# A gated linear attention with a two-layer feed-forward block: w_in issued behind a v tile, w_out in four rows a partition, turned q copied straight, and a new order

## The chip, the cores and the metric

The kernel runs on one core of a Trainium2 chip. The metric is the time of one execution on the device in microseconds (us). Three runs of the kernel before gave 192.94, 193.02 and 193.77 us, so its median is 193.02 us. One further execution was recorded by the hardware profiler; its own time was 192.63 us.

## The reference

There are four sequences (B = 4), eight heads (H = 8), 768 steps (S) and 48 numbers a head (D). For each sequence and head a 48 x 48 state is carried through the steps:

```python
f = 1.0 / (1.0 + np.exp(-f_logit))
for t in range(S):
    state = f[:, :, t, :, None] * state + np.einsum('bhd,bhe->bhde', k[:, :, t], v[:, :, t])
    y[:, :, t] = np.einsum('bhd,bhde->bhe', q[:, :, t], state)
x = y.transpose(0, 2, 1, 3).reshape(B * S, H * D)     # 3072 x 384
h = x @ w_in                                          # 3072 x 2048
out = np.maximum(0.01 * h, h) @ w_out                 # 3072 x 384
```

All inputs and the output are float32 in device memory.

## The kernel before, in words

**Tiling.** The 768 steps are cut into six chunks of 128. A unit is one chunk of one sequence, so there are 24 units, numbered chunk by chunk: units 0 to 3 are the first chunk of the four sequences. Inside a chunk the recurrence becomes matmuls. The logarithms of the gates are summed along the chunk by a triangular matmul; k and q are scaled by the exponentials of that sum; k and q are turned, so that the head's numbers lie on the partitions; k against q gives scores, which are masked to the past and multiplied with v. The state of all earlier chunks is added through another matmul and is then brought up to date. The resulting y is turned to x, and two units together (256 columns) go through the feed-forward block: `up(m, g, bk)` makes two of the 16 blocks of 128 hidden numbers for the pair m, `up_act` applies the leaky rectifier into the buffer gT, `down(u, half, bk)` multiplies half of the hidden blocks of unit u with w_out, `put` copies the result out of PSUM and `out_dma` stores it. Line 412 is the matmul of `up` and line 422 that of `down`.

**The first chunk.** Units 0 to 3 are treated as one "quad", by functions whose names begin with `q_`. Their f, k and q lie in the tiles fq, kq and qq, with four consecutive steps of a head next to each other in a partition (`load_quad`, line 69), and a partition holds every fourth row for one sequence. Each of the twelve loads has 192 KB. The quad is worked in two halves hh of four heads. `q_exp_act` and `q_ln_act` make the log gates on ScalarE, `q_gate_pe` (line 202) sums them, `q_decay_act` (line 206) takes the exponentials into emq and aq, and `q_k_scale` and `q_q_scale` (line 211) scale k and q into khq and qhq on VectorE or GpSimd. `q_turn_pe` (line 223) turns them on TensorE; `q_k_out` and `q_q_out` copy the turned tiles from PSUM to kTq and qTq and undo the four-step interleaving while they copy. `q_score_pe` (line 240) multiplies them. `q_mask` (line 251), or `q_wf_act` with `q_mask_pool`, masks the scores; `q_back_pe` and `q_back_out` turn k back for the state; `q_mix_pe` (line 257) makes y, `state_pe` (line 379) with `q_state_dve` (line 282) the state, and `y_out`, `x_pe`, `x_out` bring y into the feed-forward block's input xT.

**Loads.** Raw tiles of later units (f, k, q, v; 192 KB each, in runs of 48 float32) are issued by `load_part` (line 166) on the SP queue, in the written order; an issue that has to wait holds up all issues behind it. w_in and w_out are cast from float32 to bf16 on the way and are therefore issued from GpSimd's software queue, w_in in two halves of its columns (`load_w_in`, line 175) and w_out in four quarters of its rows (`load_w_out`, line 180). An issue on GpSimd stands in line with GpSimd's computing instructions.

**The order** of all instructions is written out by hand at the end of the function, one call a line; each engine works through its own instructions in that order, and the framework adds the waits. `idle_pe(n, bk)` (line 139) issues n matmuls on zeros. The letters V, A and G in a call mean VectorE, ScalarE and GpSimd.

Of the kernel before, what the change touches and what calls it, by code (L numbers as in the profile page):

```python
# [16 lines left out]
def kernel(  # L17
# [37 lines left out]
    def bank(i):  # L55
        return banks[i][:, :]
# [47 lines left out]
    w_in_b = const.tile([128, NK, FF], BF16, tag="w_in")  # L104
    w_out_b = const.tile([128, NF, KD], BF16, tag="w_out")
# [83 lines left out]
    qTq = [const.tile([128, 2, 4, 128], BF16, name=f"qTq{i}", tag=f"qTq{i}") for i in range(2)]  # L189
# [35 lines left out]
    def q_turn_out(dst, hh, bk, pp):  # L225
        tp = bank16(bk).rearrange("p (a j t b) -> p a b t j", a=2, j=4, b=4)
        return dict(out=dst[hh][:, pp].rearrange("p b (t j) -> p b t j", j=4), in_=tp[:, pp])

    def q_k_out(eng, hh, pp, bk):
        move(eng, **q_turn_out(kTq, hh, bk, pp))  # L230

    def q_q_out(eng, hh, pp, bk):
        move(eng, **q_turn_out(qTq, hh, bk, pp))

    def q_score_pe(hh, bp, bk0, bk1):
        pw = [bank(bk).rearrange("p (b a n) -> p b a n", b=2, a=2) for bk in (bk0, bk1)]
        for bl in range(2):
            for pp in range(2):
                for e in range(2):
                    nc.tensor.matmul(pw[e][:, bl, pp, :], kTq[hh][64 * e:64 * e + 64, pp, 2 * bp + bl, :],  # L240
                                     qTq[hh][64 * e:64 * e + 64, pp, 2 * bp + bl, :], start=True, stop=True)
# [166 lines left out]
    def up(m, g, bk):  # L408
        for i in range(2):
            for kk in range(NK):  # L410
                ff = 2 * g + i
                nc.tensor.matmul(bank(bk)[:, i * 256:(i + 1) * 256], w_in_b[:, kk, ff * 128:(ff + 1) * 128],  # L412
# [21 lines left out]

    q_exp_act(0)
    q_exp_act(1)
    q_ln_act(0)
    load_part(1, "v", v)
    q_ln_act(1)
    load_part(0, "v", v)  # L440
    load_w_in(0)
    idle_pe(40, 7)
    q_gate_pe(0, 0, 0)
    load_part(3, "v", v)
    load_w_in(1)
    q_gate_pe(0, 1, 1)
    load_part(2, "v", v)
    q_decay_act(0, 0, emq, 1.0, 0)
    q_gate_pe(1, 0, 2)
    q_decay_act(0, 0, aq, -1.0, 0)  # L450
    q_k_scale(V, 0, 0)
    q_decay_act(0, 1, emq, 1.0, 1)
    q_gate_pe(1, 1, 3)
    q_q_scale(G, 0, 0)
    q_decay_act(0, 1, aq, -1.0, 1)
    q_k_scale(V, 0, 1)
    q_decay_act(1, 0, emq, 1.0, 2)
    q_turn_pe(khq, 0, 0, 4)
    q_decay_act(1, 0, aq, -1.0, 2)
    q_end_pe(5)  # L460
    q_q_scale(V, 0, 1)
    load_part(4, "f", f_logit)
    q_k_scale(G, 1, 0)
    q_decay_act(1, 1, emq, 1.0, 3)
    q_turn_pe(khq, 0, 1, 4)
    q_q_scale(V, 1, 0)
    q_decay_act(1, 1, aq, -1.0, 3)
    q_turn_pe(qhq, 0, 0, 6)
    q_k_out(A, 0, 1, 4)
    q_k_scale(G, 1, 1)  # L470
    q_turn_pe(qhq, 0, 1, 6)
    q_k_out(V, 0, 0, 4)
    q_end_act(5)
    q_turn_pe(khq, 1, 0, 7)
    q_q_out(A, 0, 0, 6)
    q_turn_pe(qhq, 1, 0, 0)
    q_q_out(V, 0, 1, 6)
    q_q_scale(G, 1, 1)
    q_turn_pe(khq, 1, 1, 7)
    cast_v(V, 1)  # L480
    q_score_pe(0, 1, 1, 2)
    q_k_out(A, 1, 0, 7)
    q_k_out(V, 1, 1, 7)
    q_score_pe(0, 0, 3, 5)
    q_mask(0, 1, 0, 1)
    q_wf_act(0, 1, 1, 2)
    q_turn_pe(qhq, 1, 1, 0)
    q_back_pe(1, 4)
    q_wf_act(0, 0, 1, 5)
    load_part(4, "k", k)  # L490
    q_back_pe(3, 6)
    q_q_out(V, 1, 1, 0)
    q_mask_pool(0, 1, 1)
    q_back_pe(0, 7)
    q_q_out(A, 1, 0, 0)
    q_back_pe(2, 2)
    q_back_out(V, 1, 4)
    q_back_out(A, 3, 6)
    q_mask(0, 0, 0, 3)
    q_mask_pool(0, 0, 1)  # L500
    q_back_out(A, 2, 2)
    idle_pe(4, 1)
    q_score_pe(1, 0, 1, 5)
    cast_v(V, 0)
    q_back_out(A, 0, 7)
    state_pe(1, 0)
    q_score_pe(1, 1, 4, 6)
    q_mask(1, 0, 1, 5)
    q_mask(1, 0, 0, 1)
    state_pe(0, 3)  # L510
    q_mask(1, 1, 0, 4)
    idle_pe(5, 5)
    q_mix_pe(0, 2)
    q_mask(1, 1, 1, 6)
    q_mix_pe(1, 7)
    load_part(4, "q", q)
    y_out(A, 0, 2)
    y_out(V, 1, 7)
    q_state_dve(0)
    idle_pe(6, 4)  # L520
    x_pe(0, 5)
    x_pe(1, 1)
    cast_v(G, 3)
    load_part(4, "v", v)
    x_out(A, 0, 5)
    q_state_dve(1)
    q_state_pool(0)
    x_out(A, 1, 1)
    idle_pe(5, 7)
    q_mix_pe(3, 4)  # L530
    load_part(5, "f", f_logit)
    state_pe(3, 6)
    q_state_pool(1)
    up(0, 0, 2)
    y_out(A, 3, 4)
    cast_v(V, 2)
    q_state_dve(3)
    load_w_out(1)
    load_part(5, "k", k)
    up(0, 7, 7)  # L540
    up_act(0, 0, 2)
    load_w_out(0)
    q_mix_pe(2, 3)
    x_pe(3, 5)
    load_part(5, "q", q)
    up_act(0, 7, 7)
    state_pe(2, 0)
    y_out(V, 2, 3)
    up(0, 4, 1)
    q_state_pool(3)  # L550
    x_out(A, 3, 5)
    q_state_dve(2)
    up(0, 6, 4)
    load_w_out(3)
    up_act(0, 4, 1)
    x_pe(2, 6)
    gate_exp(4)
    up(0, 1, 2)
    q_state_pool(2)
    x_out(V, 2, 6)  # L560
    up_act(0, 6, 4)
    load_part(5, "v", v)
    up(0, 3, 7)
    load_w_out(2)
    gate_ln(4)
    up_act(0, 1, 2)
    up(1, 1, 3)
    up_act(0, 3, 7)
    up(1, 7, 5)
    up_act(1, 1, 3)  # L570
    up(1, 6, 0)
    up_act(1, 7, 5)
    up(1, 5, 1)
    up_act(1, 6, 0)
    load_part(6, "f", f_logit)
    cast_v(V, 4)
    gate_pe(4, 6)
    up(1, 3, 4)
    up_act(1, 5, 1)
    decay_em(4, 6)  # L580
    up(1, 2, 2)
    decay_a(4, 6)
    k_scale(V, 4)
    up(1, 0, 7)
    up_act(1, 3, 4)
    q_scale(G, 4)
    up_act(1, 2, 2)
    up(0, 5, 3)
    up_act(1, 0, 7)
    up(0, 2, 5)  # L590
    load_part(6, "k", k)
    up_act(0, 5, 3)
    turn_pe(4, 0)
    gate_exp(5)
    up(1, 4, 1)
    up_act(0, 2, 5)
    turn_k(V, 4, 0)
    gate_ln(5)
    turn_q(V, 4, 0)
    down(2, 0, 6)  # L600
    up_act(1, 4, 1)
    down(1, 0, 4)
    load_part(6, "q", q)
    gate_pe(5, 2)
    down(3, 0, 7)
    decay_em(5, 2)
    decay_a(5, 2)
    k_scale(V, 5)
    down(0, 0, 3)
    load_part(6, "v", v)  # L610
    q_scale(V, 5)
    load_part(7, "f", f_logit)
    state_pe(4, 5)
    state_dve(4)
    turn_pe(5, 0)
    load_part(7, "k", k)
    down(1, 1, 4)
    turn_k(A, 5, 0)
    turn_q(V, 5, 0)
    load_part(7, "q", q)  # L620
    cast_v(V, 5)
    score_pe(2, 1, 2, 5, 0)
    put(A, 1, 4)
    load_part(7, "v", v)
    down(0, 1, 3)
    mask(5, 0, 5)
    gate_exp(6)
    out_dma(1)
    gate_ln(6)
    mask(4, 1, 2)  # L630
    state_pe(5, 4)
    down(2, 1, 6)
    mask(4, 0, 1)
    put(A, 0, 3)
    load_part(8, "f", f_logit)
    mask(5, 1, 0)
    out_dma(0)
    gate_pe(6, 5)
    state_dve(5)
    mix_pe(4, 2)  # L640
    put(A, 2, 6)
    cast_v(G, 6)
    mix_pe(5, 3)
    decay_em(6, 5)
    load_part(8, "k", k)
    state_pool(4)
    y_out(V, 4, 2)
    down(3, 1, 7)
    decay_a(6, 5)
    y_out(V, 5, 3)  # L650
    out_dma(2)
    gate_exp(7)
    k_scale(V, 6)
    gate_ln(7)
    state_pool(5)
    load_part(8, "q", q)
    x_pe(4, 1)
    q_scale(V, 6)
    x_pe(5, 0)
    put(A, 3, 7)  # L660
    state_pe(6, 6)
    load_part(8, "v", v)
    x_out(V, 4, 1)
    x_out(A, 5, 0)
    gate_pe(7, 4)
    state_dve(6)
    turn_pe(6, 2)
    decay_em(7, 4)
    out_dma(3)
    up(2, 3, 5)  # L670
    decay_a(7, 4)
    turn_k(V, 6, 2)
    k_scale(G, 7)
    load_part(9, "f", f_logit)
    turn_q(A, 6, 2)
    cast_v(V, 7)
    up(2, 6, 3)
    q_scale(V, 7)
    up_act(2, 3, 5)
    load_part(9, "k", k)  # L680
    up(2, 0, 7)
    up_act(2, 6, 3)
    turn_pe(7, 1)
    gate_exp(8)
    load_part(9, "q", q)
    state_pe(7, 0)
    up_act(2, 0, 7)
    up(2, 4, 6)
    turn_k(V, 7, 1)
    load_part(9, "v", v)  # L690
    gate_ln(8)
    turn_q(V, 7, 1)
    up(2, 2, 4)
    state_dve(7)
    up_act(2, 4, 6)
    load_part(10, "f", f_logit)
    up(2, 1, 2)
    up_act(2, 2, 4)
    score_pe(3, 5, 3, 7, 1)
    load_part(10, "k", k)  # L700
    up_act(2, 1, 2)
    gate_pe(8, 6)
    up(2, 5, 0)
    mask(6, 1, 3)
    load_part(10, "q", q)
    decay_em(8, 6)
    cast_v(G, 8)
    decay_a(8, 6)
    up(2, 7, 4)
    mask(7, 0, 7)  # L710
    k_scale(G, 8)
    up_act(2, 5, 0)
    load_part(10, "v", v)
    down(4, 0, 2)
# [607 lines left out]
```

## Time and profile before

| what | value |
|---|---|
| median of three runs | 193.02 us |
| profiled execution, own time | 192.63 us |
| span of the profiled execution, first to last instruction | 190.8 us |
| mean granted TensorE clock | 0.982 |
| TensorE busy | 175.7 us (92%) |
| VectorE busy | 87.4 us (46%) |
| ScalarE busy | 124.1 us (65%) |
| GpSimd busy | 59.2 us (31%) |
| read from and written to device memory | 25.17 MB and 4.72 MB |

A row of the profile's groups names a line, an engine, an operation, the tiles out and in, the shape, how often it ran, its busy time and the mean length of one. Matmuls are pipelined, so the mean length of one (273 ns at line 412) is longer than the distance from one to the next. The chain of work that ended last is followed back from the last instruction; each piece of it has a start, a length and what ran. The slices cut the span into 40 equal parts of 4.77 us, each digit the busy share in tenths. Rows of busy time by window give start and end, the window's length, busy time and instructions of TensorE, its weight loads, VectorE, ScalarE and GpSimd, then the granted clock, the busy share of the 16 DMA engines and GB/s.

### The profile page before, as it was taken

To read this page: it belongs to the slowest core of one execution; us is meant where nothing else is said; L and a number is where in the kernel's file an instruction comes from. 1 tells how busy PE (TensorE), PEld (TensorE's weight loads), DVE (VectorE), ACT (ScalarE), POOL (GpSimd) and SP (SyncE) were. 2 spreads that over 40 slices of the span, in tenths; PEclk is the share of its full clock that TensorE was granted. 3 is DMA by queue.
4 is the path that set the end of the run, shared out by engine and by line. 5 is a ranking of instruction groups with operands and counts; after the bars stand their busy time and mean duration, and the time that the engine had idled before them with its cause. 6 is when DMAs were issued, how large, how long until landed. Compare 5 with 4: busy or idle time off the path is not lost.

```text
span 190.8 us, 4830 instructions
## 1 busy us (share of the span) xinstructions
PE 175.7 (92%) x1905; PEld 136.3 (71%) x1905; DVE 87.4 (46%) x193; ACT 124.1 (65%) x266; POOL 59.2 (31%) x109
## 2 busy tenths in 40 slices
PE   4952679999999999999999999999999999999992
PEld 2841459886679778768877787877668787776861
DVE  7001799313597557547556436894528304010000
ACT  2661176994479879967968778986458665642822
POOL 8000855620143644441532512844502500000000
PEclk9997599999999999999999999999999999999999
DMA  4999899999088989899999999972742490113202
GB/s 143 264 222 259 172 190 213 166 185 178 25 196 190 212 176 235 167 228 200 217 193 192 221 195 191 227 157 65 156 115 62 79 138 0 45 43 83 82 3 84
DMA packets 106679, 29.42 MB, mean 154 GB/s; under 512 B 97696, under 2 KB 105888, under 8 KB 106656
## 3 DMA queue, kind: packets, MB, share of 16 engines
q1 hardware_dynamic: 102656, 25.18, 62.2%
q0 software_dynamic: 2912, 3.15, 10.1%
q10 hardware_dynamic: 1088, 0.79, 1.3%
q8 instruction: 15, 0.25, 0.5%
q14 instruction: 8, 0.07, 0.1%
HBM read 25.17 MB, written 4.72 MB: 157 GB/s over the span
## 4 chain that ended last, share of the span: by engine, by line
PE 84%; DMA 9%; ACT 2%; SPq 1%; DVE 1%; issue 1%; POOL 1%; POOLq 0%; ACTq 0%
PE ps L412 33%; PE ps L422 33%; DMA qq<-in_q_dram 6%; PE ps L332 3%; PE ps L357 3%; DMA fq<-in_f_logit_dram 2%; PE ps L371 2%; PE ps L368 2%; PE ps L304 2%; PE ps L379 2%; PE ps L402 2%; SPq L69 1%; PE ps L139 1%; PE ps L223 1%; ACT kqh L145 1%
## 5 line engine op out<-in xcount | busy, mean ns | idle before, releaser
L412 PE MATMUL ps<-xT,w_in_b 128*128 128x256 bf16 x576 | 70.6, 273 | 0.0
L422 PE MATMUL ps<-w_out_b,gT 128*128 128x384 bf16 x384 | 68.4, 326 | 0.0
L417 ACT ACTIVATE gT<-ps 128x512 bf16<-128x512 f32 x96 | 56.8, 604 | 12.3 <-PE ps L412 10.2
L412 PEld LDWEIGHTS <-w_in_b 128*128 128x128 bf16 x576 | 54.3, 98 | 7.7
L422 PEld LDWEIGHTS <-gT 128*128 128x128 bf16 x384 | 36.2, 98 | 20.6
L361 DVE TENSOR_TENSOR wm<-ps,ut 128x512 bf16<-128x512 f32 x40 | 24.9, 682 | 14.7 <-ACT gT L417 10.4
L288 POOL CAST sb<-sf 64x192 bf16<-64x192 f32 x40 | 15.1, 378 | 35.9 <-PE ps L368 31.3
L145 ACT COPY osb<-ps 128x384 f32<-128x384 f32 x23 | 11.0, 480 | 20.7 <-PE ps L422 20.7
L319 DVE TENSOR_TENSOR kqh<-k_raw,em_t 128x384 bf16<-128x384 f32 x14 | 7.9, 567 | 12.9 <-ACT em_t L311 12.7
L323 POOL TENSOR_TENSOR kqh<-q_raw,a_t 128x384 bf16<-128x384 f32 x11 | 10.3, 938 | 10.4 <-issue 7.1
L393 POOL TENSOR_TENSOR sf<-sf,a_end 128x192 f32<-128x192 f32 x16 | 9.2, 576 | 13.1 <-DVE sf L388 12.6
L147 DVE CAST xn<-ps 128x384 bf16<-128x384 f32 x12 | 6.5, 554 | 12.6 <-ACT osb L145 7.8
L311 ACT ACTIVATE em_t<-ps 128x384 bf16<-128x384 f32 x20 | 9.8, 497 | 2.5 <-PE ps L307 2.5
L147 DVE COPY kqT<-ps 128x512 bf16<-128x512 bf16 x17 | 6.8, 421 | 8.6 <-PE ps L332 5.3
L298 ACT ACTIVATE lf<-f_raw 128x384 bf16<-128x384 f32 x20 | 10.5, 532 | 0.1
L145 ACT COPY kqT<-ps 128x512 bf16<-128x512 bf16 x11 | 6.3, 587 | 6.6 <-PE ps L332 3.8
L295 ACT ACTIVATE f_raw<-f_raw 128x384 f32<-128x384 f32 x20 | 10.4, 526 | 0.0
L139 PE MATMUL ps<-fill 128*128 128x256 bf16 x60 | 9.2, 317 | 1.1 <-DVE ind L129 1.1
L314 ACT ACTIVATE a_t<-ps 128x384 bf16<-128x384 f32 x20 | 9.9, 508 | 0.0
L145 ACT CAST xn<-ps 128x384 bf16<-128x384 f32 x12 | 5.8, 480 | 4.7 <-PE ps L371 2.9
L387 DVE TENSOR_TENSOR sf<-sf,ps 64x192 f32<-64x192 f32 x16 | 5.5, 342 | 7.1 <-PE ps L379 4.2
L139 PEld LDWEIGHTS <-fill 128*128 128x128 bf16 x60 | 6.7, 114 | 2.8 <-issue 1.3
(88 smaller groups left out, 194.1 us busy)
## 6 DMA issues: line engine op xcount, KB each, us to landing
v_raw<-in_v_dram SPq DMA_DIRECT2D x24, 192.0 KB, 4.0
out_dram<-osb SPq DMA_DIRECT2D x24, 192.0 KB, 2.5
f_raw<-in_f_logit_dram SPq DMA_DIRECT2D x20, 192.0 KB, 3.9
k_raw<-in_k_dram SPq DMA_DIRECT2D x20, 192.0 KB, 4.0
q_raw<-in_q_dram SPq DMA_DIRECT2D x20, 192.0 KB, 4.0
w_in_b<-in_moe_w_in_dram POOLq DMA_DIRECT2D x2, 768.0 KB, 12.2
w_out_b<-in_moe_w_out_dram POOLq DMA_DIRECT2D x4, 384.0 KB, 8.6
qq<-in_q_dram SPq DMA_DIRECT2D x4, 192.0 KB, 12.1
```

The source lines that it names most:

```text
L139: nc.tensor.matmul(bank(bk)[:, 0:256], fill[:, 0:128], fill[:, 0:256], start=True, stop=True)
L145: eng.copy(out=out, in_=in_)
L147: eng.tensor_copy(out=out, in_=in_)
L288: nc.gpsimd.tensor_copy(out=state_b[b][r, :, e * D:(e + 1) * D], in_=state_f[b][r])
L295: nc.scalar.activation(raw[u]["f"], raw[u]["f"], AF.Exp, scale=-1.0)
L298: nc.scalar.activation(lfs[u % R_LF][:, :, 0:D], raw[u]["f"], AF.Ln, bias=1.0)
L314: nc.scalar.activation(a_ts[u % R_EM], bank(bk)[:, 0:H * D], AF.Exp, scale=-1.0)
L323: eng.tensor_mul(qhs[u % R_KQS][:, :, 0:D], r["q"], a_ts[u % R_EM])
L361: nc.vector.tensor_mul(wms[e][u % R_WM], bank(bk).rearrange("p (i n) -> p i n", i=P2), ut[:, None, :].to_broadcast([128, P2, 128]))
L412: nc.tensor.matmul(bank(bk)[:, i * 256:(i + 1) * 256], w_in_b[:, kk, ff * 128:(ff + 1) * 128], xTs[m % R_XT][:, kk].rearrange("p a n -> p ...
L417: nc.scalar.activation(gTs[m % GBUFS][:, 2 * g:2 * g + 2].rearrange("p f a n -> p (f a n)"), bank(bk), AF.Prelu, alpha=0.01)
L422: nc.tensor.matmul(bank(bk)[:, 0:KD], gTs[u // 2 % GBUFS][:, ff, u % 2, :], w_out_b[:, ff, :], start=(ff == 0), stop=(ff == NF - 1))
```

## The change

Six things change together.

1. **First loads.** The loads of k for sequences 2 and 3 move from ScalarE's queue to SP's, and ScalarE loads its activation table right after its two loads of f.
2. **w_in.** `load_w_in(0)` stood right behind the first activations in the written order, the first thing in GpSimd's queue after the constants. Now a new instruction, `touch('v')`, copies one column of the raw v tile of unit 1 on GpSimd; it waits for that tile, and both issues of w_in stand behind it. The v tiles of the first chunk are now issued in the order 2, 0, 1, 3.
3. **Turned q.** `q_q_out` copies a turned q from PSUM as it lies; the interleaving of the four steps is undone by the stride with which the score matmuls read q.
4. **w_out.** A partition takes four consecutive rows of w_out in each quarter, where it took one row of each of four blocks.
5. **w_in's columns.** To match, `up` takes every fourth column of w_in as the weights of a matmul, where it took 128 neighbouring ones.
6. **Order.** The hand-written order is new throughout: the second half of heads comes first, all four units of the first chunk come before the first `up`, and the fillers are 52 where there were 60.

```diff
     first_load(nc.sync, "k", 0)
-    first_load(nc.scalar, "k", 2)
+    nc.scalar.preload_act_table_set("natural_log_exp_and_others")
     first_load(nc.sync, "k", 1)
-    first_load(nc.scalar, "k", 3)
+    first_load(nc.sync, "k", 2)
+    first_load(nc.sync, "k", 3)
     first_load(nc.sync, "q", 0)
-    nc.scalar.preload_act_table_set("natural_log_exp_and_others")
...
+    w_in_p = w_in_b.rearrange("p a (g n i) -> p a g n i", n=128, i=4)
...
+    seen = const.tile([128, 1], FP32, tag="seen")
+
+    def touch(what):
+        src = {"f": fq[:, 0, 0, 0:1], "k": kq[:, 0, 0, 0:1], "q": qq[:, 0, 0, 0:1],
+               "v": raws["v_raw"][1][:, 0, 0:1], "w": raws["v_raw"][3][:, 0, 0:1]}[what]
+        nc.gpsimd.tensor_copy(out=seen, in_=src)
...
-                            in_=moe_w_out.rearrange("(a p) n -> p a n", p=128)[:, g * w:(g + 1) * w, :])
+                            in_=moe_w_out.rearrange("(g p i) n -> p g i n", p=128, i=w)[:, g, :, :])
...
-    qTq = [const.tile([128, 2, 4, 128], BF16, name=f"qTq{i}", tag=f"qTq{i}") for i in range(2)]
+    qTq = [const.tile([128, 2, 512], BF16, name=f"qTq{i}", tag=f"qTq{i}") for i in range(2)]
...
     def q_q_out(eng, hh, pp, bk):
-        move(eng, **q_turn_out(qTq, hh, bk, pp))
+        move(eng, qTq[hh][:, pp], bank16(bk).rearrange("p (a n) -> p a n", a=2)[:, pp])
...
+                    nc.tensor.matmul(bank((bk0, bk1)[e])[:, i * 128:(i + 1) * 128], kTq[hh][r, pp, b, :],
+                                     qTq[hh][r, pp].rearrange("p (j t b) -> p b t j", j=4, b=4)[:, b], start=True, stop=True)
...
-                nc.tensor.matmul(bank(bk)[:, i * 256:(i + 1) * 256], w_in_b[:, kk, ff * 128:(ff + 1) * 128],
+                nc.tensor.matmul(bank(bk)[:, i * 256:(i + 1) * 256], w_in_p[:, kk, ff // 4, :, ff % 4],
```

The start of the new order, as GpSimd and SP see it:

```diff
+    load_part(2, "v", v)
+    load_part(0, "v", v)
+    load_part(1, "v", v)
+    load_part(3, "v", v)
+    q_q_scale(G, 1, 0)
...
+    q_q_scale(G, 0, 0)
+    q_q_scale(G, 0, 1)
+    cast_v(G, 2)
+    touch('v')
+    cast_v(G, 1)
+    load_w_in(0)
+    load_w_in(1)
+    q_mask_pool(1, 1, 1)
+    q_mask_pool(0, 1, 1)
...
+    up(1, 3, 7)
```

More of the change, by code (lines that the diff above doesn't have):

```diff
@@ L623 @@
[L623 to L641 removed]
+    put(A, 0, 1)
+    down(1, 1, 3)
+    cast_v(V, 5)
+    turn_q(A, 5, 0)
+    turn_k(V, 5, 0)
+    out_dma(0)
+    gate_exp(6)
+    state_pe(5, 2)
@@ new lines @@
+    load_part(11, "k", k)
+    decay_a(8, 4)
+    down(4, 0, 3)
+    mask(6, 0, 0)
+    k_scale(G, 8)
+    up_act(2, 5, 2)
+    q_scale(V, 8)
+    load_part(11, "q", q)
+    mix_pe(6, 1)
+    mask(7, 1, 7)
+    cast_v(G, 9)
+    state_pe(8, 5)
+    load_part(11, "v", v)
+    down(4, 1, 3)
+    mask(7, 0, 6)
+    state_pool(6)
+    y_out(A, 6, 1)
+    gate_exp(10)
+    state_dve(8)
+    load_part(12, "f", f_logit)
+    gate_ln(10)
+    x_pe(6, 4)
+    turn_pe(8, 0)
+    put(A, 4, 3)
+    x_out(V, 6, 4)
@@ L937 @@
[L937 to L958 removed]
+    load_part(17, "k", k)
+    up(4, 1, 7)
@@ new lines @@
+    up_act(4, 2, 2)
+    turn_q(V, 12, 3)
+    mix_pe(10, 4)
+    gate_ln(14)
+    turn_k(V, 12, 3)
+    load_part(17, "q", q)
+    state_pe(11, 1)
+    cast_v(G, 15)
+    up_act(4, 1, 7)
+    down(6, 0, 6)
+    mask(11, 1, 5)
+    state_pool(10)
+    y_out(A, 10, 4)
+    state_dve(11)
+    load_part(17, "v", v)
+    gate_ln(15)
+    down(8, 0, 0)
+    load_part(18, "f", f_logit)
+    x_pe(10, 2)
+    load_part(18, "k", k)
+    down(6, 1, 6)
+    x_out(A, 10, 2)
+    load_part(18, "q", q)
+    gate_pe(13, 3)
@@ new lines @@
+    turn_q(V, 15, 1)
+    turn_k(A, 15, 1)
+    down(11, 0, 5)
+    up_act(6, 5, 0)
+    score_pe(7, 4, 3, 7, 2)
+    up(6, 0, 6)
+    mask(15, 0, 7)
+    state_pe(15, 1)
+    up(6, 6, 0)
+    mask(15, 1, 2)
+    gate_exp(19)
+    cast_v(G, 19)
+    up_act(6, 0, 6)
+    cast_v(G, 18)
+    up(6, 7, 7)
+    state_dve(15)
+    up_act(6, 6, 0)
+    mix_pe(15, 2)
+    mask(14, 0, 4)
+    gate_exp(18)
+    down(12, 0, 6)
+    up_act(6, 7, 7)
+    state_pool(15)
+    y_out(V, 15, 2)
+    gate_ln(18)
+    mask(14, 1, 3)
@@ new lines @@
+    gate_pe(16, 1)
+    x_pe(15, 0)
+    down(12, 1, 6)
+    decay_em(16, 1)
+    x_out(V, 15, 0)
+    gate_ln(19)
+    k_scale(V, 16)
+    decay_a(16, 1)
+    mix_pe(14, 4)
+    load_part(22, "k", k)
+    q_scale(V, 16)
+    put(A, 12, 6)
+    gate_pe(18, 7)
+    state_pe(16, 2)
+    state_pool(14)
+    y_out(A, 14, 4)
+    down(10, 0, 3)
+    out_dma(12)
+    decay_em(18, 7)
+    state_dve(16)
+    load_part(22, "q", q)
+    decay_a(18, 7)
+    k_scale(V, 18)
+    x_pe(14, 0)
+    q_scale(G, 18)
@@ new lines @@
+    turn_pe(16, 1)
+    x_out(A, 14, 0)
+    gate_pe(17, 6)
+    down(11, 1, 5)
+    turn_k(V, 16, 1)
+    turn_q(A, 16, 1)
+    turn_dma(18)
+    decay_em(17, 6)
+    decay_a(17, 6)
+    k_scale(V, 17)
+    up(7, 7, 4)
+    put(A, 11, 5)
+    q_scale(G, 17)
+    load_part(23, "k", k)
+    up(7, 5, 2)
+    up_act(7, 7, 4)
+    out_dma(11)
+    state_pe(17, 7)
+    up(7, 6, 0)
+    load_part(23, "q", q)
+    up_act(7, 5, 2)
+    state_dve(17)
+    turn_pe(17, 1)
+    up_act(7, 6, 0)
+    up(7, 2, 6)
@@ new lines @@
+    turn_k(V, 17, 1)
+    turn_q(A, 17, 1)
+    up(7, 4, 5)
+    up_act(7, 2, 6)
+    up(7, 3, 4)
+    up_act(7, 4, 5)
+    score_pe(8, 2, 7, 0, 1)
+    up_act(7, 3, 4)
+    up(7, 0, 6)
+    mask(17, 0, 0)
+    down(13, 0, 5)
+    mask(16, 1, 7)
+    cast_v(G, 21)
+    up_act(7, 0, 6)
+    cast_v(G, 20)
+    gate_exp(21)
+    mask(16, 0, 2)
+    gate_exp(20)
+    up(7, 1, 4)
+    mask(17, 1, 1)
+    gate_ln(21)
+    state_pe(18, 0)
+    gate_ln(20)
+    mix_pe(16, 6)
+    state_dve(18)
+    up_act(7, 1, 4)
@@ new lines @@
+    down(10, 1, 3)
+    state_pool(16)
+    y_out(A, 16, 6)
+    x_dma(16)
+    mix_pe(17, 7)
+    put(A, 10, 3)
+    down(15, 0, 2)
+    state_pool(17)
+    y_out(A, 17, 7)
+    out_dma(10)
+    x_dma(17)
+    gate_pe(19, 1)
+    down(15, 1, 2)
+    decay_em(19, 1)
+    decay_a(19, 1)
+    k_scale(V, 19)
+    gate_pe(21, 4)
+    q_scale(G, 19)
+    gate_pe(20, 0)
+    put(A, 15, 2)
+    down(14, 0, 6)
+    decay_a(20, 0)
+    out_dma(15)
+    decay_a(21, 4)
+    turn_dma(19)
+    q_scale(V, 20)
@@ new lines @@
+    mix_pe(23, 5)
+    y_out(V, 22, 0)
+    up(10, 4, 7)
+    y_out(A, 23, 5)
+    x_dma(22)
+    up(10, 1, 1)
+    up_act(10, 4, 7)
+    x_dma(23)
+    up(10, 5, 4)
+    up_act(10, 1, 1)
+    up(10, 6, 2)
+    up_act(10, 5, 4)
+    up(9, 3, 6)
+    up_act(10, 6, 2)
+    down(20, 0, 3)
+    up_act(9, 3, 6)
+    down(21, 0, 0)
+    down(19, 0, 5)
+    down(18, 0, 7)
+    down(19, 1, 5)
+    down(18, 1, 7)
+    put(A, 19, 5)
+    out_dma(19)
+    down(20, 1, 3)
+    put(A, 18, 7)
+    out_dma(18)
```

1303 lines of the change are left out of this document (550 added, 753 removed).

## The prediction

> **What bounds the kernel now.** I read the page's busy slices first, then the chain that ended last, the DMA queues in two windows of the start, the busy times by window, and last the groups of TensorE and VectorE that the change touches.
>
> The slices: TensorE is full from the seventh slice (one is 4.77 us) to the end, and the clock is granted in full there. What can be won lies in the first 31 us.
>
> ```profile
> PE   4952679999999999999999999999999999999992
> DVE  7001799313597557547556436894528304010000
> PEclk9997599999999999999999999999999999999999
> DMA  4999899999088989899999999972742490113202
> ```
>
> The chain in order of time (start, length, what): TensorE, VectorE and GpSimd stand still for q. It is asked for up to 7.25 and has landed at 19.28.
>
> ```profile
> 7.25 12.03 DMA qq<-in_q_dram
> ...
> 24.72 0.68 DVE wm L251
> ...
> 31.44 1.31 PE ps L412 x12
> ...
> 34.77 3.93 PE ps L412 x36
> ```
>
> DMA queues, first from 5 to 10 us, then from 10 to 15 us (packets, MB, share of 16 engines): the software queue q0, which carries only w_in here, takes over half and then five sixths of the engines.
>
> ```profile
> q0 software_dynamic: 234, 0.48, 53.8%
> ...
> q0 software_dynamic: 401, 0.79, 84.1%
> ```
>
> With 32.2% from 15 to 20 us, w_in costs 2.69 + 4.21 + 1.61 = 8.5 us of all 16 engines (4.25 a half), inside the wait for q. The same view gives other prices: 0.75 MB of quads in the first 5 us took 49.9% of them, 2.5 us, so four quad tiles (0.79 MB) cost 2.6 us; from 20 to 31 us a raw tile costs 1.0 us (2.13 MB in 98.5% of 11 us); w_out from 31 to 46 us costs 71.7% of 15 us, 10.75 us.
>
> Busy times by window: after q has landed VectorE is the pace, 10.14 of 11.2 us. Then TensorE has no gap.
>
> ```profile
> 14.00:20.00 6.00, 1.02 (x24) 0.85 (x24) 1.62 (x4) 0.67 (x2) 0.55 (x1) 0.76 1.06 237
> 20.00:31.20 11.20, 9.22 (x133) 7.54 (x134) 10.14 (x19) 5.62 (x11) 7.13 (x9) 0.82 0.99 194
> 31.20:46.00 14.80, 14.80 (x154) 12.55 (x151) 4.90 (x12) 11.90 (x25) 6.47 (x13) 1.00 1.20 184
> ```
>
> **The change, part by part.** Profiled run: span 190.8, own time 192.63, so 1.83 lies around the span; the median of the runs, 193.02, is 0.39 above it.
>
> *q without w_in.* First data moves at 2.3 us; f, k and q cost 3 x 2.6 = 7.8 us of the engines and then end at about 10.1. The last q is issued at about 7.3 to 7.9 (SP now issues two k tiles more, but its q issue waited for f until 4.96 anyway) and a first-load tile took 3.9 us to land: 11. So q lands at 10 to 11 instead of 19.28, and it no longer decides: the decays on ScalarE (L206) start at 10.11, because the gate matmuls follow the 40 idle matmuls and these stay. Their third ends at 10.86 + 0.50 = 11.36, and there VectorE can scale q. ScalarE's table load moves ahead, which gains nothing behind those matmuls.
>
> *VectorE's way to the first up.* In the new order all four first units are finished before the first `up`, so more stands on VectorE ahead of it. From 11.4, by rows: four scalings at 0.55 = 2.2; casts of v0 and v3 at 0.36 = 0.7; two turned k at 0.68 = 1.4; two turned q, now straight, at 0.41 as the straight kqh copy = 0.8 (0.69 before, so 0.55 is saved on this chain); six masks at 0.68 = 4.1; states of two units at 0.75 = 1.5; y of units 2 and 0 at 0.55 = 1.1; x of unit 2 at 0.36. Sum 12.2, and 0.65 of waiting for ScalarE's copies of the same tiles: the first `up` could start at 24.2. ScalarE and GpSimd lie beside it: GpSimd scales q until 14.3 (0.92 each, the third when its decay ends at 13.28), casts v2 and v1, and masks from 17.3 (2 x 1.15, done at 19.6, before the matmuls that need them at 20.5).
>
> *The wait in front of w_in.* `touch` needs v1, the third v tile in SP's order. SP issues the v tiles from 8 us on, each when a k tile has landed; four cost 4 us of the engines and land from 12 to 14, so the wait itself is about hidden behind GpSimd's scaling. Queued behind it on GpSimd are the cast of v1, both w_in issues (0.93 and 0.78), two masks and w_out. The first w_in issue comes at 15.6. In the profile 1.9 us passed from issue (3.07) to packets; then a half takes 4.25/0.85 = 5.0 us at the share that q0 had (84.1% here, 89.1% when w_out ran against raw tiles from 36 to 40 us), and about 0.8 to land: 23.3 and 28.3. The first half is needed at 24.2, the second by the seventh `up`, 6 x 0.66 later: 28.2. So w_in just fits. At a share of 60% (71.7 of 71.7 + 47.1, q0 and q1 from 31 to 46 us) a half takes 7.1 us, the second lands at 32.5, and 4.2 us are lost. Ends 0 and 4.2; I take 1.5, nearer the first, since two rows speak for it.
>
> *w_out, four rows a partition.* Four times fewer and longer pieces. Bounds: 10.75 us as now, or 8.5 us, w_in's price for as many bytes. It is issued from about 28, behind w_in. The first `down` comes 15 `up` and 0.9 of other matmuls after the first, at 36 to 37; two quarters at 4.25/0.85 land at about 35 to 36, the rest at 40, when the second halves start. Lost: 0 to 2, taken 0.5.
>
> *w_in in steps of four.* 576 weight loads now read every fourth column, and 576 times anything counts. Loads of neighbouring columns, one after another, come every 28 ns (16 of L264 in 0.51 us, the last 0.096) and hide below matmuls that come every 109 ns (6 in 0.66). The nearest row for a step is VectorE's copy: 0.68 stepped, 0.41 straight, 1.65 times. 28 x 1.65 = 46 ns hides: cost 0. The other end takes the recorded 98 ns as the price: 162, 53 over, times 576 = 30 us. I take 0, as the spacing shows what a load really holds up; no row excludes the other end.
> The Trainium skill has two rules here. "Advanced Engine Details and Errata", Memory Cachelines, says that SBUF is read in 16-byte lines and needs two hits on a line: a step of four bf16 still makes two, so by it the sum stays as it is; no run here shows it yet. "TensorE: Matmul & The Clock Gate", Weight-path perf modes, has the fast weight load also for stepped columns; without it a load takes by that page an estimated 107 ns (128/1.2), which the 109 ns still cover.
>
> *Turned q in steps.* The 32 score matmuls (L240, 8 in 0.40 us) read q 256 bytes apart. At 1.65 times it is +0.26 a call; the first call is on the way, others lie below masks: 0 to 1.0, taken 0.3.
> By the same Cachelines section one hit on a line pays, by an amount that it does not state: the rule speaks against this edit, and the term would be above 0, as taken.
>
> *The sum.* At 34.60 before, 24 `up` matmuls and all of the first four units are done, one gate (0.4) is not; the last matmul ends at 187.4: 152.8 later. After the first `up` of the new order there remain 152.8 + 24 x 0.109 + 0.17 (one x) - 0.4 = 155.2, then 3.4 of copying and storing: 158.6. The old equivalent start is 190.8 - 158.6 = 32.2. The new: 24.2 + 1.5 + 0.5 + 0.3 = 26.5. Span 185.1, own time 186.9, against the median of runs 187.3. The rest of the order has the same matmuls, up to 8 idle ones fewer; I cost it at nothing, since TensorE is gapless in both halves of the profile; if the new order leaves gaps, nothing covers them.
>
> **The rivals.**
> *DMA is the next bound.* Now w_in, w_out and raw tiles follow each other closely. Up to 46 us the engines worked 12.2 + 6.4 + 11.1 + 17.8 = 47.5 us (share times window) and had then loaded everything through unit 7. The new kernel needs 45.2 of it by 46 - 5.7 = 40.3, while 38 us at 1.1 give 42. If this stops TensorE, 3.4/1.1 = 3 us go back, or w_in at 60% does the same: 190 to 192. Against it: unit 7 is first used at 55, and at 46 to 56 the share fell to 0.45.
> *w_in comes much too late and the change does nothing.* If the halves take 7.1 us and w_out loses its 2, with 1 for the scores: 24.2 + 7.2 = 31.4, 192.2. Speaks for it: the old halves needed 10.2 and 14.1 us to land; against it: that was with quads beside them on two queues.
> *Slower: the stepped weights show.* The place is L412, the price (load - 109 ns) x 576; it cancels the gain of 5.7 at 119 ns a load, and at 162 ns gives 217. For it: the recorded 98 ns; against it: the spacing of 28.
>
> **How the numbers follow.** Half a per cent, 1 us, is about what these runs can tell from no change. My forecast (184.0 to 189.8) 0.58; DMA bound (189.8 to 192) 0.17; no gain 0.06; slower 0.19, of which 0.13 for the weights and 0.06 for gaps in the new order. Faster 0.75, same 0.06, slower 0.19. The range 184 to 192 leaves out the slower cases and the equal ones' upper part; its low end is no stall at all (24.2, 185.0) and 1 us for earlier loads.
>
> **What would show it.** q landing by 11; VectorE scaling q at 11.4; w_in's landings near 23 and 28; first L412 at 24 to 26, with gaps in front of the seventh `up` if w_in is late; L412 still at 0.66 us for 6; L240 above 0.40 for 8; q0 with some 1536 fewer packets. L412 at over 0.70 for 6 or gaps on TensorE after 40 us would make it wrong.

## The result, and the profile after

The changed kernel takes 195.24 us (median of four runs, 194.94 to 195.56), the kernel before 193.06 us beside it. The ratio is 1.0105, with a 95% interval of 1.0081 to 1.013: slower by about 1%, where 187.3 us was forecast. The profiled execution took 195.56 us, its span 193.8 us. Medians and ranges here and below are of all runs of a kernel; the ratios leave out the few runs that took over 1.5% longer than the fastest of the same kernel.

The slices of the page, as shown for before (one is now 4.85 us):

```profile
PE   4988956999999999999999999999999998999992
DVE  6058981022474694878158418526228705100000
PEclk9999995799999999999999999999999999999999
DMA  5998999993498989799998997670491263202202
```

TensorE's hole has become shallower and has moved. Before, it stood in the third and fourth slice (10 to 19 us) and waited for q. Now it stands in the sixth and seventh (24 to 34 us), and in the seventh and eighth (29 to 39 us) the granted clock falls as well. The chain in order of time (start, length, what) names the cause:

```profile
17.17 0.88 POOL w_in_b L183
18.05 12.78 DMA w_in_b<-in_moe_w_in_dram
30.87 1.25 PE ps L418 x5
32.13 0.32 PE ps L408 x3
32.45 7.81 PE ps L418 x54
...
156.50 3.01 PE ps L418 x28
159.51 2.34 DMA xT<-xn
161.98 3.44 PE ps L418 x30
```

L418 is the matmul of `up` (L412 before). Where the chain ran through q's loading until 19.28, it now runs through w_in's second half until 30.83. Behind it 54 matmuls take 7.81 us, 145 ns each, where 36 took 3.93 us before, 109 ns each. Late in the kernel there is a stop that the old order did not have, for two turns by DMA. The timeline shows the moment of the wait (start, busy time, what; in brackets the idle time before and what ended it):

```profile
26.72 0.27 PE L418 MATMUL ps<-xT,w_in_b 128*128 128x256 bf16 x1
...
30.87 0.78 PEld L418 LDWEIGHTS <-w_in_b 128*128 128x128 bf16 x5 [4.24 <-DMA w_in_b<-in_moe_w_in_dram]
30.87 1.25 PE L418 MATMUL ps<-xT,w_in_b 128*128 128x256 bf16 x5 [3.88 <-DMA w_in_b<-in_moe_w_in_dram]
```

The issues of w_in and the time to landing (the first half is issued at 17.1 us and lands at 26.3, the second at 18.0 and 30.8):

```profile
L183 POOL DMA_DIRECT2D w_in_b<-in_moe_w_in_dram x2: 786/862/937, 17.1 to 18.0; - x2
...
DMA to landing us min/median/max: 9.2/11.0/12.8
```

One matmul of the first `up` runs, and the second one waits four microseconds. The first `up` reads hidden blocks 6 and 7, which lie in the first half of w_in; that half had landed, as the first matmul proves. The built kernel's list of instructions on TensorE tells why: the second weight load waits for the second half's semaphore (DMASW1), a counter that this transfer raises when it has landed. In the kernel before, that wait stands in front of the seventh pair of load and matmul, the first that reads the second half.

```
487 L418 Ldweights w_in_b [waits DVE_49,DMASW0_49]
488 L418 Matmult ps_71<-xT_217,w_in_b 128x256 [waits Activation_49]
489 L418 Ldweights w_in_b [waits DMASW1_49]
490 L418 Matmult ps_71<-xT_217,w_in_b 128x256
```

In a partition's row of 6144 elements of w_in_b, the second half's pieces begin at 1024 and end at 6143, with pieces of the first half between them. The first weight load reads every fourth element from 514 to 1022, ahead of all of them; the second reads from 2562 to 3070, between them, and touches none. This fits a framework that compares a stepped read with a transfer by their two ends alone; no run tests that.

Three parts of the profile are as forecast. q landed 4.0 us after its issue at 5.1 to 7.0, at 11 us, and the decays were what scaling waited for next. Six `up` matmuls at full clock still take 0.66 us. q0, the software queue, has 1376 packets where it had 2912, which is 1536 fewer. The rows of the tiles qq and kq (scalings by engine: count, ns min/median/max; then, for qq, the time to landing):

```profile
L219 POOL TENSOR_TENSOR qhq<-qq,aq x3: 913/954/990, 12.1 to 14.4; 128x384 bf16<-128x384 f32 x3
L219 DVE TENSOR_TENSOR qhq<-qq,aq x1: 995/995/995, 12.4 to 12.4; 128x384 bf16<-128x384 f32 x1
...
DMA to landing us min/median/max: 4.0/4.0/4.2
```

```profile
L219 DVE TENSOR_TENSOR khq<-kq,emq x4: 559/1056/1262, 11.6 to 15.7; 128x384 bf16<-128x384 f32 x4
```

VectorE's scalings, 0.56 us where GpSimd is silent, took 0.85 to 1.26 us where GpSimd works beside them.

The account from the forecast span of 185.1 to 193.8: the dense stretch of `up` began, net of the one matmul done, at 30.76 instead of 26.5 (+4.3). The granted clock (last column but two) fell in this wait:

```profile
25.00:30.00 5.00, 1.96 (x35) 1.51 (x34) 3.23 (x9) 2.03 (x6) 4.46 (x10) 0.94 1.14 209
30.00:35.00 5.00, 4.13 (x21) 2.96 (x22) 0.71 (x2) 1.19 (x2) 1.48 (x3) 0.50 1.06 192
```

It was 0.50 from 29.4 to 36.2 us, and this is what is called a cold clock below. The 59 `up` matmuls and three turns behind the wait took 1.25 + 0.32 + 7.81 = 9.38 us, where they take 59 x 0.109 + 0.17 = 6.6 at full clock (+2.8). The stop for the DMA turns cost about 0.9: 36 matmuls from 156.50 end at 160.43; the scores (0.55) start 0.27 late, and the next `up` 0.67 late. A stretch paced by ScalarE from 59.7 to 65.4 cost 0.3. The remaining 0.4 us of the 8.7 was not traced.

### The profile page after: what moved, and what is told of

It is laid out like the page before. It is cut to its first block, busy times and chain, and to the rows that moved or that the text cites. A ratio compares the mean times of both kernels' runs of the same rounds, so it can differ in the third digit from the quotient of the medians.

```text
span 193.8 us, 4812 instructions
## 1 busy us (share of the span) xinstructions
PE 180.6 (93%) x1897; PEld 143.4 (74%) x1897; DVE 86.2 (44%) x186; ACT 126.3 (65%) x271; POOL 57.9 (30%) x112
## 3 DMA queue, kind: packets, MB, share of 16 engines
q0 software_dynamic: 1376, 3.15, 8.8%
## 4 chain that ended last, share of the span: by engine, by line
PE 82%; DMA 8%; ACT 5%; POOL 3%; issue 0%; DVE 0%; POOLq 0%; ACTq 0%
PE ps L428 32%; PE ps L418 32%; DMA w_in_b<-in_moe_w_in_dram 7%; PE ps L140 4%; PE ps L338 3%; PE ps L363 2%; PE ps L377 2%; PE ps L374 2%; ACT gT L423 2%; PE ps L310 2%; PE ps L385 1%; PE ps L408 1%; DMA xT<-xn 1%; ACT emq L214 1%; ACT aq L214 1%; POOL v_b L148 1%
## 5 line engine op out<-in xcount | busy, mean ns | idle before, releaser
L418 PE MATMUL ps<-xT,w_in_b 128*128 128x256 bf16 x576 | 72.5, 279 | 4.7 <-DMA w_in_b<-in_moe_w_in_dram 3.9
L418 PEld LDWEIGHTS <-w_in_b 128*128 128x128 bf16 x576 | 62.0, 115 | 8.3 <-DMA w_in_b<-in_moe_w_in_dram 4.2
L428 PEld LDWEIGHTS <-gT 128*128 128x128 bf16 x384 | 36.2, 98 | 21.0
L367 DVE TENSOR_TENSOR wm<-ps,ut 128x512 bf16<-128x512 f32 x40 | 25.4, 682 | 18.3 <-PE ps L363 14.4
L146 ACT COPY osb<-ps 128x384 f32<-128x384 f32 x22 | 10.6, 482 | 25.4 <-PE ps L428 25.2
L294 POOL CAST sb<-sf 64x192 bf16<-64x192 f32 x40 | 14.6, 364 | 25.6 <-PE ps L374 23.1
L148 POOL CAST v_b<-v_raw 128x384 bf16<-128x384 f32 x15 | 8.5, 578 | 18.3 <-PE ps L313 11.6
L325 DVE TENSOR_TENSOR kqh<-k_raw,em_t 128x384 bf16<-128x384 f32 x15 | 9.8, 651 | 8.7 <-ACT em_t L317 8.5
L399 POOL TENSOR_TENSOR sf<-sf,a_end 128x192 f32<-128x192 f32 x16 | 8.6, 536 | 9.7 <-PE ps L374 6.1
L148 DVE CAST xn<-ps 128x384 bf16<-128x384 f32 x10 | 5.5, 554 | 6.7 <-PE ps L377 4.2
L338 PE MATMUL ps<-ident,kqh 128*128 128x128 bf16 x112 | 8.4, 219 | 0.0
```

What stands on the lines that cost most here:

```text
L146: eng.copy(out=out, in_=in_)
L148: eng.tensor_copy(out=out, in_=in_)
L294: nc.gpsimd.tensor_copy(out=state_b[b][r, :, e * D:(e + 1) * D], in_=state_f[b][r])
L338: nc.tensor.transpose(tp[:, i, p, :], src[:, 2 * p:2 * p + 2, :], ident)
L367: nc.vector.tensor_mul(wms[e][u % R_WM], bank(bk).rearrange("p (i n) -> p i n", i=P2), ut[:, None, :].to_broadcast([128, P2, 128]))
L418: nc.tensor.matmul(bank(bk)[:, i * 256:(i + 1) * 256], w_in_p[:, kk, ff // 4, :, ff % 4], xTs[m % R_XT][:, kk].rearrange("p a n -> p (a n) ...
```

## The experiments

The theory was that the framework's wait, and the cold clock after it, ate the gain. Its rivals were that the engines are simply short of data, that the stepped weights cost, or that deferring w_in is worth nothing.

**w_in in two tiles.** The stepped view of one tile is what the wait hangs on; with a tile for each half it cannot.

```diff
-    w_in_b = const.tile([128, NK, FF], BF16, tag="w_in")
-    w_in_p = w_in_b.rearrange("p a (g n i) -> p a g n i", n=128, i=4)
+    w_in_h = [const.tile([128, NK, FF // 2], BF16, name=f"w_in{g}", tag=f"w_in{g}") for g in range(2)]
+    w_in_p = [t.rearrange("p a (g n i) -> p a g n i", n=128, i=4) for t in w_in_h]
...
-        nc.gpsimd.dma_start(out=w_in_b[:, :, g * w:(g + 1) * w],
+        nc.gpsimd.dma_start(out=w_in_h[g],
...
-                ... w_in_p[:, kk, ff // 4, :, ff % 4],
+                ... w_in_p[ff // 8][:, kk, ff // 4 % 2, :, ff % 4],
```

> The changed kernel with w_in kept in two tiles, one for each half of its columns, so that the first six `up` wait for the first half alone. Theory (the stepped view of one tile makes the framework hold the second weight load for the second half): six `up` run from 26.7 to 30.7, the second half has just landed (30.8), the clock stays full, and about 4 us of standing and 2.8 us of cold clock come back: 188 to 189.5 us. Rival (the engines are short of data anyway, or the first half also lands only shortly before 30.8): under 2 us come back, 193.5 or more. Rival (stepped weights are what costs): no change, 195.

189.67 us (188.76 to 189.95), ratio to before 0.9798 (0.9769 to 0.9828): 0.2 us above the expected range. In the built kernel the wait for the second half now stands at the seventh `up`, and that half, landed at 29.4, was there in time. The timeline of this run:

```profile
27.12 0.82 PE L418 MATMUL ps<-xT,w_in 128*128 128x256 bf16 x6
...
27.95 6.27 PE L418 MATMUL ps<-xT,w_in 128*128 128x256 bf16 x54
...
42.59 1.46 PE L428 MATMUL ps<-w_out_b,gT 128*128 128x384 bf16 x8 [0.31 <-DMA w_out_b<-in_moe_w_out_dram]
```

The first `up` runs through, and 54 matmuls take 6.27 us, where the same view of the changed kernel has 8.01, at full clock. Of the 195.24 us, 5.6 are gone with an edit that leaves the order of the instructions and the size of the transfers as they were. Both rivals are out, under 2 us for a shortage of data and no change for the stepped weights. The next thing that is late is w_out, by 0.3 us.

**Neighbouring columns again.** The edits of w_in's columns and w_out's rows are undone; one tile, and the rest as changed.

```diff
-                            in_=moe_w_out.rearrange("(g p i) n -> p g i n", p=128, i=w)[:, g, :, :])
+                            in_=moe_w_out.rearrange("(a p) n -> p a n", p=128)[:, g * w:(g + 1) * w, :])
...
-                ... w_in_p[:, kk, ff // 4, :, ff % 4],
+                ... w_in_b[:, kk, ff * 128:(ff + 1) * 128],
```

> The changed kernel with neighbouring columns of w_in as weights again and w_out loaded row by row again; w_in is still one tile and still issued behind the v tile. Theory (the lost time is the wait for the second half): as with two tiles, 188 to 189.5 us, since the read of neighbouring columns is not held for the second half; w_out's four times as many pieces may cost up to 2 us of it. Rival (stepped weight loads cost time on TensorE): clearly below the kernel with two tiles, by 1 us or more.

192.18 us (191.0 to 194.77), 0.9927 (0.9888 to 0.9967). The first `up` came at 27.46 without a stop, although the second half landed only at 28.9, so it is the step in the view, not one tile as such, that brings the wait forward. The run is 2.5 us slower than two tiles and 0.7 above the expected range, the 2 us allowed for w_out included. It shows no gain from straight weights; what is late is w_out in four times as many pieces:

```profile
44.88 1.46 PE L428 MATMUL ps<-w_out_b,gT 128*128 128x384 bf16 x8 [2.31 <-DMA w_out_b<-in_moe_w_out_dram]
```

The wait is 2.0 us longer than the one with two tiles, so the four rows a partition are worth about 2 us here, where w_out's loading has no slack left. The other half microsecond was not traced.

**The wait filled with idle matmuls.**

```diff
     x_out(A, 0, 6)
+    idle_pe(34, 7)
     up(1, 3, 7)
```

> The changed kernel with 34 idle matmuls in front of the first `up`, to fill the wait for w_in. Theory: the wait itself stays (first `up` at about 30.8), but the clock stays full, and 54 + 5 `up` matmuls run at 109 ns instead of 145 and 250: 2.5 us come back, 192.5 us. Rival (the slow matmuls are slow for another cause, as DMA writing beside them): no change, 195.

192.69 us (191.84 to 192.79), 0.9952 (0.9935 to 0.997): 2.55 us below the changed kernel, where 2.5 was expected. The data is no earlier (the first `up` starts at 30.72), and yet the clock stays full:

```profile
27.01 3.88 PE L140 MATMUL ps<-fill 128*128 128x256 bf16 x34
...
30.72 0.82 PE L418 MATMUL ps<-xT,w_in_b 128*128 128x256 bf16 x6
...
31.54 6.06 PE L418 MATMUL ps<-xT,w_in_b 128*128 128x256 bf16 x54
```

```profile
30.00:35.00 5.00, 5.00 (x50) 4.92 (x48) 0.72 (x2) 2.98 (x5) 2.13 (x4) 1.00 0.81 146
```

The slow matmuls were slow from the clock: with DMA at work beside them as well (181 GB/s from 30 to 35 us) they keep their pace in the run with two tiles, whose clock is full there. The wait and its aftermath are thus separated: 2.5 us for the clock, about 3 for the standing.

**Stepped columns in the kernel before.** Only the edits of `up` and `load_w_out`, in the old order.

```diff
-                ... w_in_b[:, kk, ff * 128:(ff + 1) * 128],
+                ... w_in_p[:, kk, ff // 4, :, ff % 4],
...
-                            in_=moe_w_out.rearrange("(a p) n -> p a n", p=128)[:, g * w:(g + 1) * w, :])
+                            in_=moe_w_out.rearrange("(g p i) n -> p g i n", p=128, i=w)[:, g, :, :])
```

> The kernel before with the stepped columns of w_in and the four rows a partition of w_out, nothing else. w_in has landed long before its first use there, so only the pace of the weight loads and w_out's loading are seen. Theory (stepped loads hide below the matmuls): 192.3 to 193.3 us, six `up` matmuls still in 0.66 us. Rival (stepped loads cost): 1 us or more slower, at 2 ns a load 194.2.

193.70 us (193.29 to 194.71), 1.0018 (0.9997 to 1.0039): no difference that can be told from the 193.37 us of the kernel before beside it, though the median lies 0.4 above the range that the theory gave. The weight loads of w_in and 36 `up` matmuls in this run:

```profile
L413 PEld LDWEIGHTS <-w_in_b x576: 111/114/136, 32.1 to 182.8; 128*128 128x128 bf16 x192
...
35.44 4.09 PE L413 MATMUL ps<-xT,w_in_b 128*128 128x256 bf16 x36
```

A stepped load is recorded at 114 ns instead of 98, and 36 matmuls take 4.09 us, as in the kernel before. The stepped loads hide; a cost of up to 0.75 us, the upper end of the interval, is not excluded by the times.

**q undone while copying, as before**, on top of two tiles: `q_q_out` and the operand of the scores as in the kernel before.

```diff
-        move(eng, qTq[hh][:, pp], bank16(bk).rearrange("p (a n) -> p a n", a=2)[:, pp])
+        tp = bank16(bk).rearrange("p (a j t b) -> p a b t j", a=2, j=4, b=4)
+        move(eng, qTq[hh][:, pp].rearrange("p b (t j) -> p b t j", j=4), tp[:, pp])
...
-                ... qTq[hh][r, pp].rearrange("p (j t b) -> p b t j", j=4, b=4)[:, b], ...
+                ... qTq[hh][r, pp, b, :], ...
```

> Two tiles for w_in, and q copied from PSUM with the interleaving undone while copying, as before; the score matmuls read neighbouring columns again. Theory (a stepped moving operand halves TensorE's pace): 16 score matmuls in about 0.87 us at full clock instead of 1.95; VectorE's two copies of q take 0.69 instead of 0.41; the scores are on the way to the masks, so the first `up` comes 0.5 to 1.5 us earlier: 188 to 189.2 us. Rival (the scores hide below VectorE, which then pays 0.55 more): 189.7 to 190.3.

189.51 us (189.06 to 190.06), 0.9807 (0.9777 to 0.9836), against 189.67: neither theory. The score matmuls themselves, first of the changed kernel, then of this run (ns min/median/max):

```profile
L246 PE MATMUL ps<-qTq,kTq x32: 377/398/399, 17.4 to 21.3; 64*128 64x128 bf16 x32
```

```profile
L247 PE MATMUL ps<-qTq,kTq x32: 213/216/227, 16.9 to 19.7; 64*128 64x128 bf16 x32
```

One takes 398 ns with the step and 216 without. They come in pairs, one for each half of the rows. At full clock a stepped pair follows the other after 224 ns, a straight pair after 55 ns: four times the distance. (The 0.87 us for 16 in the kernel before, on which the expectation rests, fell for the most part into a time of half clock; in this run one call of 16 took 0.62 us.) The stepped read costs TensorE more than was thought, the straight copy saves VectorE 0.3 us each, and the first `up` comes at 27.15 us here and at 27.12 with two tiles alone: the end does not move.

**w_in issued first again**, on top of two tiles.

```diff
+    load_w_in(0)
+    load_w_in(1)
     q_exp_act(1)
...
-    touch('v')
...
-    load_w_in(0)
...
-    load_w_in(1)
```

> Two tiles for w_in, without the touch of v, and w_in issued first on GpSimd's queue as in the kernel before. Theory (w_in beside the first loads is what held q up): q lands at 18 to 20 instead of 11, VectorE scales q only then, the first `up` comes at 33 to 35 and the kernel takes 195 to 197 us. Rival (the quads' loads are late for another cause and the wait in front of w_in does nothing): as with two tiles alone, 189.7.

197.33 us (196.88 to 198.56), 1.0202 (1.0172 to 1.0233). The landing of q, then the first `up`:

```profile
DMA to landing us min/median/max: 12.2/12.5/13.0
```

```profile
36.04 0.82 PE L418 MATMUL ps<-xT,w_in 128*128 128x256 bf16 x6
```

The wait in front of w_in does what it should: without it q takes 8.5 us longer to land, the first `up` comes 9 us later, and the kernel is 7.7 us slower, a little more than expected (195 to 197). Not all of that need be the wait for q: the granted clock was 0.50 from 16 to 33 us in this trace. With w_in first the new order is 4 us worse than the old one; that it puts all four units ahead of the first `up` is the likely reason, which no run isolates.

**All but the first scaling of q on VectorE**, on top of two tiles.

```diff
-    q_q_scale(G, 0, 0)
+    q_q_scale(V, 0, 0)
...
-    q_q_scale(G, 0, 1)
+    q_q_scale(V, 0, 1)
```

> Two tiles for w_in, and the second and third scaling of q, which GpSimd does, given to VectorE. Theory (VectorE and GpSimd slow each other when they scale at the same time: 0.55 alone and up to 1.26 together): VectorE does six scalings at 0.55 in less time than four contended ones now, the first turned copies come 0.5 us earlier and the kernel takes 189 us. Rival (VectorE's work is simply longer): two scalings more, 1.1 us later, 190.8.

189.32 us (188.1 to 189.43), 0.9781 (0.9744 to 0.9818), which overlaps with two tiles alone: at most a small gain, and not the theory's shorter time on VectorE either. VectorE had five scalings and now has seven; they took 5.2 us in all where the five had taken 4.9. It was not 1.1 us longer, so the rival's 190.8 is out.

**Both of the last edits to q together.**

> Two tiles for w_in, q undone while copying, and all but the first scaling of q on VectorE. If the two edits add up as the theories have it: 187.5 to 188.5 us. If VectorE is what paces this stage (both rivals): 190.5 to 191.5.

189.37 us (188.61 to 190.94), 0.9809 (0.9756 to 0.9862). Neither of the two sums: they do not add up. What paces the stage from 12 to 27 us beyond the one engine or the other stays open in part. One thing that the traces show is the clock. From the end of the last scaling on VectorE to the start of the first `up` (in the run with idle matmuls, to the first of these), 10.2 us pass in the changed kernel's trace and 10.4 in that of the tenth experiment, where the clock is full in this stage; in the seven others with the new order and w_in deferred, where it is 0.50 for 3.4 to 6.8 us, 11.2 to 12.0 pass. For the run with two tiles:

```profile
20.00:25.00 5.00, 5.00 (x63) 3.96 (x59) 3.52 (x8) 3.29 (x8) 1.84 (x3) 0.59 1.09 195
```

That is about 1 us, more than the last three kernels differ by from the one with two tiles. What decides whether the clock falls there is not shown.

**The old order with w_in deferred.**

```diff
-    load_w_in(0)
...
-    load_w_in(1)
...
     q_q_scale(G, 1, 1)
+    load_w_in(0)
+    load_w_in(1)
```

> The kernel before, its own order and all, with both issues of w_in moved behind GpSimd's last scaling of q (no touch, no other edit). Theory: q lands at 11 and the first `up` is ready at about 24, but the old order wants the second half of w_in in its second `up`, and that half lands at 28 to 30, so TensorE stands and cools there: 190.5 to 192 us, between the kernel before and the changed one with two tiles. Rival (deferring w_in is worth nothing without the new order, or its masks on GpSimd come too late behind the issues): 193 or more. Rival (deferring is worth its full 8 us in the old order too): 187 or less.

192.16 us (191.43 to 193.68), 0.9951 (0.9921 to 0.9981), 0.2 us above what the theory gave. The timeline shows the first `up`, and the second:

```profile
24.95 0.82 PE L412 MATMUL ps<-xT,w_in_b 128*128 128x256 bf16 x6
...
29.75 1.46 PE L412 MATMUL ps<-xT,w_in_b 128*128 128x256 bf16 x6 [3.97 <-DMA w_in_b<-in_moe_w_in_dram]
```

The first `up` comes 6 us earlier than before, and the second, which truly reads the second half, stands for it and then runs cold (6 in 1.46 us). The new order avoids this wait, since its first six `up` ask for one half. That it gains by this is not shown by itself: with w_out in the same small pieces it takes 192.18 us (second experiment), and the old order 192.16. The 189.67 us are reached with w_out's long pieces besides.

**The late stop taken out**, on top of two tiles and VectorE's scaling.

```diff
     mix_pe(21, 3)
-    turn_dma(22)
...
     y_out(A, 21, 3)
-    out_dma(17)
     x_dma(21)
+    turn_dma(22)
+    out_dma(17)
...
-    score_pe(11, 3, 1, 2, 5)
...
     up(10, 2, 4)
+    score_pe(11, 3, 1, 2, 5)
```

The masks of units 22 and 23 follow the scores, and their two `mix_pe` go behind three more `up`.

> Two tiles for w_in, all but the first scaling of q on VectorE, and late in the kernel the scores of units 22 and 23 put three `up` later, with the DMA turn of x of unit 21 issued ahead of the one of k and q of unit 22. Theory (TensorE stands 1 us at about 155 for these two DMA turns): 188.2 to 188.7 us, about 1 us below the kernel without this last edit. Rival (what follows only moves to a later wait): 189.3.

188.64 us (188.18 to 191.55), 0.9748 (0.9725 to 0.977). The chain of its profiled execution runs from 153.40 without a stop:

```profile
153.40 5.89 PE ps L418 x54
159.30 0.55 PE ps L363 x16
159.85 3.40 PE ps L418 x30
```

So the stop is gone. That it gains is not shown: the interval overlaps with that of the run with VectorE's scaling, 189.32 us. The profiled execution was the one of 191.55 us; in it TensorE waited 3.3 us for w_out, which had been 0.3 us late with two tiles alone. Why w_out came so late in this one is not known.

**w_out issued earlier**, on top of that.

```diff
     q_state_pool(0)
+    load_w_out(0)
+    load_w_out(1)
...
     k_scale(G, 4)
+    load_w_out(3)
+    load_w_out(2)
```

> The kernel of the run before (two tiles for w_in, q scaled on VectorE, scores of units 22 and 23 later), with the first two quarters of w_out issued right behind GpSimd's copy of unit 0's state and the other two behind its scaling of k of unit 4, 5 and 2 us earlier. Theory (w_out's last quarters now land just when the second half of a `down` wants them, 0.3 us late with two tiles alone and 3.3 us late in the profile of the run before): no wait of TensorE for w_out, 187.5 to 188.3 us, and a smaller spread. Rival (w_out ahead takes the engines from the raw tiles of units 4 to 6, which are then late): 188.6 or more.

188.78 us (187.97 to 191.29), 0.9744 (0.971 to 0.9779): the same as the run before within the intervals, so the edit is not shown to gain, and the spread has not become smaller. The time is the one that the rival gave (188.6 or more), but in the profile TensorE waits for no raw tile. The wait for w_out is gone there too, where 32 matmuls of `down` follow each other:

```profile
38.78 5.20 PE ps L428 x32
```

The last two kernels are about 2.5% faster than the kernel before and 3.4% faster than the changed one (188.64 against 195.24).

## Why the prediction was wrong

**What bounded the kernel** was read rightly: w_in beside the first loads held q up, and the way back in the sixth experiment costs 7.7 us. q landed at 11, as the sum had it.

**The step that failed** is in the paragraph on the wait in front of w_in: "The first half is needed at 24.2, the second by the seventh `up`". The second half was needed by the second matmul of the first `up`. The prediction took from the code which columns an `up` reads and never asked which waits the framework makes of a stepped view. The landings were bounded only in part: the second half came at 30.8, within 28.3 to 32.5, the first at 26.3, later than 23.3 and also than the 25.4 at 60%. Its issue came at 17.1 instead of 15.6, behind scalings on GpSimd that ended at 15.4 instead of 14.3, and the 1.9 us from issue to packets was misread: the software queue's first packet moves 3.2 us after the issue in the trace before and 2.5 us after it here. With the need at the seventh `up` the same landings would have cost little, which is what two tiles show at 189.67, just inside the likeliest case's 184.0 to 189.8 and 2.4 above its 187.3. Errors cancel there: the first `up` came at 27.1 instead of 24.2, and the 1.5 us taken for w_in were not lost.

**The clock was not in the sum.** The prediction had a rival in which w_in comes late and priced it by the standing alone, 192.2 us. In the four microseconds of standing the granted clock fell to 0.50, from 29.4 to 36.2 us, and that cost 2.8 us by the trace and 2.55 by the run with idle matmuls. This is what carried the time past the kernel before. Before, too, the clock had fallen while q was awaited (0.61 from 20 to 25 us), but there TensorE had only short turns to do; now the hole lies in front of dense work. The Trainium skill, "TensorE: Matmul & The Clock Gate", What's actually happening, says that the clock falls to half after an idle window of about 3.4 us. The trace agrees that standing lowers it, but not in the length: it fell 2.4 us after the last matmul had ended. And with two tiles it was 0.50 from 17.3 to 24.1 us, with no stop of over 0.6 us on TensorE in the 14 us before. So standing is one way to the cold clock here and not the only one.

**VectorE's way to the first `up`** was 24.2 and came to 26.7. Four scalings at 0.55 made 2.2 us; there are five of them on VectorE in the new order, four of k and one of q, and they took 0.56 + 0.99 + 3.22 = 4.8. The row for it stood in the profile before, where q's two scalings took 0.91 on average beside GpSimd, and I used the uncontended row of k. The gates also began 1.0 us later, since the same 40 idle matmuls took 7.41 us instead of 6.40; VectorE, whose first scaling is one of k, still began at 11.6, where 11.4 was forecast.

**The stepped operands.** The weights were costed at nothing, and that held: 1.0018 in the kernel before. The rival that had most of the chance for slower is out. For the scores I took 1.65 times from VectorE's copies; the distance of the matmuls became four times (224 ns a pair against 55 at full clock). In the end neither that nor the saved copies showed in the time. The Trainium skill, "Advanced Engine Details and Errata", Memory Cachelines, says that two hits on a line of 16 bytes are needed for full pace. The trace agrees in sign: with one hit a score matmul takes 398 ns instead of 216, and with two the weights keep the pace of the matmuls, though a load is recorded at 114 ns instead of 98.

**w_out** was bounded by 10.75 and 8.5 us and had 0.5 us of loss. TensorE waited 0.3 us for it with two tiles and 2.3 with the four rows undone: right.

**"The rest of the order ... I cost it at nothing"** was wrong by 0.9 us for the stop at the DMA turns, and by 0.3 at ScalarE's stretch. The prediction had given gaps in the new order a chance of 0.06 and no price.

## What to carry to other kernels

When a transfer is moved to land just in time, look up in the built kernel which instruction waits for it: a stepped view of one tile can wait for transfers that it does not read, and a tile for each transfer mends this. Price a wait in front of dense matmuls by its length and by the cold clock behind it. An edit that saves 8 us in one place is worth only what the next wait lets through: q came 8 us earlier, and the best kernel here is 4.7 us faster.

## What the runs showed of the hardware

- A weight load of every fourth column is recorded at 114 ns instead of 98 and does not slow matmuls of 256 columns that come every 109 ns; a moving operand whose neighbours lie 256 bytes apart takes 398 ns instead of 216 for 128 columns, and a pair of such matmuls follows the other after 224 ns instead of 55.
- 34 idle matmuls in a wait of 4 us made the program 2.55 us faster.
- The granted clock fell to 0.50 2.4 us after TensorE had stopped (changed kernel), and also without a stop of over 0.6 us (two tiles, 17.3 to 24.1 us).
- VectorE's scaling of 384 elements goes from 0.56 to up to 1.26 us beside GpSimd's, and GpSimd's from 0.92 to up to 1.29.
- The same 40 idle matmuls at the start took 5.84 to 7.45 us over the thirteen profiled executions (6.40 in the kernel before, 7.41 in the changed one).
